# Written order on all engines, a new first stage for batch 0, and batch 1's q turned by TensorE, in a Linformer attention + maxout FFN kernel

## The chip, the cores and the metric

The kernel runs on one core of one Trainium2 chip. The metric is the time of one execution in microseconds (us). Lower is better. A kernel is timed in several rounds beside the kernel before, on the same chip. Runs are marked slow (a lower granted clock than the fast ones of the same kernel, and a time over 1.5% above the fastest). Ratios are taken from fast runs alone. "Span" is the time from the first to the last instruction in the profiled execution; it is about 2 us shorter than the time of that run. Engines: PE is TensorE's matmuls, PEld its weight loads, DVE is VectorE, ACT ScalarE, POOL GpSimd, SP the engine that issues to the hardware DMA queue.

## The reference

```python
# q, k, v: (8 batches, 8 heads, 1024, 64) fp32; E, F: (64, 1024); w1..w3: (512, 768); w_out: (768, 512)
k_proj = np.einsum('ks,bhsd->bhkd', E, k)
v_proj = np.einsum('ks,bhsd->bhkd', F, v)
attn = softmax(q @ k_proj^T / 8)            # over 64 projected keys
x = (attn @ v_proj) as (8192 tokens, 512)   # 1024 tokens per batch
out = max(x @ w1, x @ w2, x @ w3) @ w_out   # (8192, 512) fp32
```

## The kernel before: the parts that matter

TensorE works through the FFN of batch b, and between its steps it does the attention of batch b+1. One FFN batch is two halves ("chunks") of 512 tokens. Each half is six `up` steps of 12 matmuls and two `down` halves of 12. A `plan` says after which step which piece of attention comes. Only TensorE keeps the order in which the program is written. The framework that builds the program orders the other engines by its own estimate:

```python
ctx.enter_context(tc.manual_schedule(engines={mybir.EngineType.PE}))
...
def load(b):                                    # one buffer each for q, k, v
    dma = nc.gpsimd.dma_start(out=q_t, in_=view(q, b))   # waits for the transpose of batch b-1
    ...
    nc.gpsimd.dma_start(out=k_t, in_=view(k, b))         # fp32 in HBM, cast to bf16 on the way
    nc.gpsimd.dma_start(out=v_t, in_=view(v, b))

def q_by_dma(b):
    q_p = att.tile([P, NPAIR, SI, 2, D], BF16, name="q_p", bufs=1)
    for g in range(NPAIR):
        nc.vector.tensor_copy(out=q_p[:, g]..., in_=qkv[b][0][...])      # four VectorE copies
    qTs[b] = att.tile([P, NPAIR * SI, P], BF16, name="qT")               # two buffers
    last_T[b] = nc.sync.dma_start_transpose(out=qTs[b], in_=q_p...)

def up(b, ch, jt):
    ...                                          # 3 x 4 matmuls into three PSUM banks
    nc.scalar.copy(out=h1s, in_=h_ps[0])
    nc.vector.tensor_tensor(out=m12, in0=h_ps[1], in1=h1s, op=ALU.max)
    nc.vector.tensor_tensor(out=hTs[b, ch][:, jt, :], in0=h_ps[2], in1=m12, op=ALU.max)

def plan(b):
    ...
    (0, 0): [qd(n)],       # n = b + 1: q_by_dma(n) after the first up step of batch b
    (0, 2): [kv(n)], ...   # k and v projections
    (0, 3): [kt(n), ld(n + 1)], ...
```

The two maxima of `up` free the PSUM banks, and so let TensorE go on. If VectorE stands still, TensorE stops a few steps later.

The softmax here doesn't subtract the row's maximum and nothing guards it: scores larger than these inputs give would overflow.

## Time and profile before

| | before |
|---|---|
| time at the start, median of 3 | 464.06 us (460.72 to 464.39) |
| span of the profiled run | 460.0 us |
| PE, DVE, ACT busy | 88%, 43%, 44% |
| first FFN matmul | 28.2 us |
| end of batch 0 | 113.7 us |
| batches 1 to 7 | 50.8, 49.7, 51.8, 53.9, 47.2, 47.3, 41.4 us |

The end of a batch is the modelled end of its last `down` matmul in the timeline of PE. Batch 7 is shorter because there is no batch 8 to do attention for.

The windows view of the kernel before, two lines of one stretch each: busy us of each engine with the number of instructions, then granted clock, DMA share and GB/s. First batch 4, then batch 6:

```profile
266.00:319.90 53.90, 50.00 (x276) 22.95 (x274) 24.11 (x40) 24.27 (x47) 1.75 (x2) 0.94 0.57 123
...
367.10:414.40 47.30, 47.30 (x276) 21.11 (x274) 23.04 (x36) 24.27 (x46) 0.00 (x0) 1.00 0.11 46
```

The same 276 matmuls keep TensorE busy without a gap in batch 6 and leave 3.9 us open in batch 4; the other 2.7 us that batch 4 is longer are matmuls at a lower clock (0.94 on average against 1.00). Undisturbed, a batch takes 47.3 us, all of it TensorE.

VectorE's largest waits in the kernel before (engine, line, whom it waited for: us in total, times, longest):

```profile
DVE q_p L141 <- DMA q_t<-in_q_dram: 74.6, 7, 12.8
DVE xT L268 <- ACT zi L258: 35.9, 28, 2.7
```

The timeline of VectorE around one of the seven waits (start, duration, what; in brackets the idle time ahead of it and what ended it):

```profile
160.72 1.29 DVE L268 TENSOR_TENSOR xT<-bank,zi 128x512 bf16<-128x512 f32 x2 [1.21 <-ACT zi L258]
172.50 1.43 DVE L141 COPY q_p<-q_t 128x1024 bf16<-128x1024 bf16 x4 [10.49 <-DMA q_t<-in_q_dram]
173.85 0.69 DVE L294 TENSOR_TENSOR m_1421<-bank,h1s 128x512 f32<-128x512 f32 x1
```

VectorE stands 10.5 us before the four copies of a q that is still on its way. Batch 2's FFN began at 164.4 us; its first maxima (line 294) stand behind the copies until 173.9, although their matmuls were done at about 167. Two lines of PE's timeline show what this does to TensorE in batch 0 and in batch 2:

```profile
93.76 0.64 PE L225 MATMUL bank<-qT,kpT 64*64 64x512 bf16 x4 [14.14 <-DVE kpT L190]
...
174.59 1.06 PE L172 MATMUL bank<-k_t,eT 128*64 128x256 bf16 x16 [2.29 <-DVE m_1421 L294]
```

The chain of waits (start, us, what) shows why the load was late:

```profile
203.10 5.57 DMA qT<-q_p
208.70 0.04 POOLq L126
208.74 0.79 issue
209.55 13.15 DMA q_t<-in_q_dram
222.76 0.30 issue
223.07 1.09 DVE q_p L141 x3
224.16 0.61 DVE m_1919 L294
```

A q load starts when the preceding DMA transpose is done, and takes 13 us; then come the copies, then the FFN's maximum that had waited behind them.

### The profile page before, as it was taken

The page shows a single profiled execution, that of the slowest core. Times are in us where ns is not written, and L with a number is a line of the kernel's source. Part 1 is how long each engine was busy: PE and PEld are TensorE (multiplying, and loading weights), DVE is VectorE, ACT ScalarE, POOL GpSimd, SP SyncE. Part 2 cuts the span into 40 slices and gives each one's busy share as a digit, 9 for nine tenths or more (in the row PEclk, how much of TensorE's full clock was granted, in tenths as well). Part 3 has the DMA queues.
Part 4 walks back from the last instruction along what each step waited for, and adds up shares of the span by engine and source line. Part 5 has one row for each costly group of instructions (what it writes and reads, how often), then busy time and mean ns, then how long its engine had stood idle before and what let it go on. Part 6 is the DMA issues. An engine that isn't in the chain of part 4 may idle for free.

```text
span 460.0 us, 5849 instructions
## 1 busy us (share of the span) xinstructions
PE 406.3 (88%) x2272; PEld 181.7 (39%) x2272; DVE 197.2 (43%) x328; ACT 200.4 (44%) x377; POOL 33.0 (7%) x45
## 2 busy tenths in 40 slices
PE   1799298089889998999799988999999999999996
PEld 1334034034434444444444435444544454444442
DVE  1233234045273608362544607354535454554251
ACT  1434251049145633574155622656265625562322
POOL 6430000200100001000100001000100000000000
PEclk9999789579999999999899997999999999999999
DMA  8999867995892496727392485805391110101102
GB/s 142 197 194 207 146 120 167 167 172 137 157 164 93 91 184 89 187 66 131 89 173 91 97 179 81 179 27 152 52 198 48 46 47 19 74 27 65 62 30 92
DMA packets 67116, 53.33 MB, mean 116 GB/s; under 512 B 33168, under 2 KB 62608, under 8 KB 67088
## 3 DMA queue, kind: packets, MB, share of 16 engines
q0 software_dynamic: 33136, 28.31, 41.5%
q1 hardware_dynamic: 33952, 24.64, 16.7%
q8 instruction: 17, 0.28, 0.2%
q14 instruction: 11, 0.09, 0.1%
HBM read 57.15 MB, written 16.78 MB: 161 GB/s over the span
## 4 chain that ended last, share of the span: by engine, by line
PE 60%; DMA 29%; issue 4%; DVE 3%; ACT 2%; POOL 0%; POOLq 0%; DVEq 0%
PE bank L284 39%; DMA q_t<-in_q_dram 19%; PE bank L305 13%; DMA qT<-q_p 8%; PE bank L242 3%; DMA k_t<-in_k_dram 2%; PE bank L172 2%; PE bank L198 2%; PE bank L225 2%; DVE q_p L141 1%; ACT pT L235 1%; DVE hT L295 0%; ACT zl L256 0%; PE bank L156 0%; ACT zi L258 0%
## 5 line engine op out<-in xcount | busy, mean ns | idle before, releaser
L284 PE MATMUL bank<-xT,w_sb 128*128 128x512 bf16 x1152 | 266.1, 387 | 2.7 <-DVE m_950 L294 1.8
L284 PEld LDWEIGHTS <-w_sb 128*128 128x128 bf16 x1152 | 111.5, 99 | 148.3 <-issue 24.6
L292 ACT COPY h1s<-bank 128x512 f32<-128x512 f32 x96 | 56.4, 589 | 102.6 <-PE bank L284 82.1
L305 PE MATMUL bank<-wout_sb,hT 128*128 128x512 bf16 x384 | 85.8, 380 | 0.0
L235 ACT ACTIVATE pT<-bank 128x512 bf16<-128x512 f32 (+1 forms) x72 | 39.2, 598 | 48.3 <-PE bank L225 48.2
L268 DVE TENSOR_TENSOR xT<-bank,zi 128x512 bf16<-128x512 f32 x64 | 41.3, 686 | 36.3 <-ACT zi L258 35.9
L305 PEld LDWEIGHTS <-hT 128*128 128x128 bf16 x384 | 36.4, 98 | 47.9 <-issue 6.2
L256 ACT ACTIVATE zl<-bank 128x512 f32<-128x512 f32 x64 | 35.1, 597 | 42.7 <-PE bank L242 42.1
L312 ACT COPY o_sb<-bank 128x512 f32<-128x512 f32 x64 | 36.9, 593 | 27.9 <-PE bank L305 27.9
L141 DVE COPY q_p<-q_t 128x1024 bf16<-128x1024 bf16 x28 | 10.3, 422 | 74.6 <-DMA q_t<-in_q_dram 74.6
L258 ACT ACTIVATE zi<-zl 128x512 f32<-128x512 f32 x64 | 37.1, 632 | 0.0
L225 PE MATMUL bank<-qT,kpT 64*64 64x512 bf16 x128 | 16.3, 409 | 14.6 <-DVE kpT L190 14.4
L172 PE MATMUL bank<-k_t,eT 128*64 128x256 bf16 x128 | 10.8, 323 | 14.4 <-DMA k_t<-in_k_dram 5.3
L242 PE MATMUL bank<-pT,vp 64*64 64x512 bf16 x128 | 14.7, 396 | 9.1 <-DVE m_436 L294 8.6
L211 ACT CAST vp<-bank 64x256 bf16<-64x256 f32 x16 | 5.8, 364 | 33.8 <-PE bank L198 19.5
L242 PE MATMUL bank<-pT,ones 64*64 64x512 bf16 x128 | 17.6, 411 | 1.8 <-ACT pT L235 1.8
L126 POOL DMA_DIRECT2D q_t<-in_q_dram x7 | 6.1, 876 | 179.2 <-DVE hT L295 91.3
L172 PEld LDWEIGHTS <-eT 128*64 128x64 bf16 x128 | 8.5, 127 | 17.3 <-issue 17.2
L134 POOL DMA_DIRECT2D k_t<-in_k_dram x7 | 6.1, 876 | 103.7 <-PE bank L172 103.5
L213 DVE CAST vp<-bank 64x256 bf16<-64x256 f32 x16 | 6.8, 427 | 14.1 <-ACT vp L211 13.9
L225 PEld LDWEIGHTS <-kpT 64*64 64x64 bf16 x128 | 4.4, 109 | 20.8 <-DVE kpT L190 15.5
L242 PEld LDWEIGHTS <-ones 64*64 64x64 bf16 x128 | 4.8, 105 | 17.1 <-issue 17.0
(224 smaller groups left out, 203.5 us busy)
## 6 DMA issues: line engine op xcount, KB each, us to landing
out_dram<-o_sb SPq DMA_DIRECT2D x30, 512.0 KB, 2.7
k_t<-in_k_dram POOLq DMA_DIRECT2D x8, 1024.0 KB, 9.4
v_t<-in_v_dram POOLq DMA_DIRECT2D x7, 1024.0 KB, 13.5
q_t<-in_q_dram POOLq DMA_DIRECT2D x7, 1024.0 KB, 12.9
w_sb<-in_moe_w_dram POOLq DMA_DIRECT2D x6, 256.0 KB, 9.0
q_t<-in_q_dram POOLq DMA_DIRECT2D x2, 512.0 KB, 15.0
v_t<-in_v_dram POOLq DMA_DIRECT2D x2, 512.0 KB, 14.7
out_dram<-o_sb SPq DMA_DIRECT2D x4, 256.0 KB, 2.0
```

The costliest lines, as they stand in the source:

```text
L141: nc.vector.tensor_copy(out=q_p[:, g].rearrange("p si h d -> p h si d"), in_=qkv[b][0][:, 2 * g:2 * g + 2],)
L172: nc.tensor.matmul(out=ps[hh * HALF:(hh + 1) * HALF, 0:4 * D], lhsT=eT[:, si, :], rhs=qkv[b][1][:, 4 * hh:4 * hh + 4, si, :], start=(si == ...
L225: nc.tensor.matmul(out=sc[hp][c * HALF:(c + 1) * HALF, :], lhsT=kpTs[b][rows, g % 2, g // 2, :], rhs=qTs[b][rows, lo:lo + SPC, :], start=T ...
L235: nc.scalar.activation(out=pTs[b, g][r, hp, :], in_=sc[hp][r], func=AF.Exp, scale=scale)
L242: nc.tensor.matmul(out=dst[hp * HALF:(hp + 1) * HALF, :], lhsT=w(rows, hp), rhs=pTs[b, g][rows, hp, :], start=True, stop=True,)
L256: nc.scalar.activation(out=zl, in_=z[c], func=AF.Ln)
L258: nc.scalar.activation(out=zi, in_=zl, func=AF.Exp, scale=-1.0)
L268: nc.vector.tensor_tensor(out=xTs[b][:, g, c * SPC:(c + 1) * SPC, :].rearrange("a si p -> a (si p)"), in0=av[c], in1=zis.pop((b, g, c)), o ...
L284: nc.tensor.matmul(out=h_ps[i], lhsT=w_sb[i][:, ct, jt * P:(jt + 1) * P], rhs=rhs_x[:, ct, :, :], start=(ct == 0), stop=(ct == NCT - 1),)
L292: nc.scalar.copy(out=h1s, in_=h_ps[0])
L305: nc.tensor.matmul(out=o_ps, lhsT=hTs[b, ch][:, jt, tt * P:(tt + 1) * P], rhs=wout_sb[:, jt, :], start=(jt == 0), stop=(jt == NJT - 1),)
L312: nc.scalar.copy(out=o_sb[:, t, :], in_=o_ps)
```

## The change

The intent was to take the DMA-bound start apart (loads of batch 0 without a cast on the way, worked on by halves of the heads, with dummy matmuls to hold TensorE's clock), to turn batch 1's q by TensorE instead of copies and a DMA transpose, and to put every engine in written order. The diff, cut to its core:

```diff
-    ctx.enter_context(tc.manual_schedule(engines={mybir.EngineType.PE}))
+    ctx.enter_context(
+        tc.manual_schedule(engines={ET.PE, ET.DVE, ET.Activation, ET.Pool, ET.SP})
+    )
 ... (batch 0: fp32 loads through SP's queue)
+        nc.sync.dma_start(out=e_f, in_=E)
+        for i in range(2):
+            q_dma = nc.sync.dma_start(out=q_f[i], in_=view(q, 0)[:, hs[i], 0:SPC])
+        for i in range(2):
+            nc.sync.dma_start(out=k_f[i], in_=view(k, 0)[:, hs[i]])
+        nc.sync.dma_start(out=f_f, in_=F)
+        for i in range(2):                      # v still cast by GpSimd's queue, after q
+            dma = nc.gpsimd.dma_start(out=v_t[:, hs[i]], in_=view(v, 0)[:, hs[i]])
+            if i == 0:
+                after(dma, q_dma)
 ... (then weights, second half of q; its own casts, transposes, scores, sums, values)
+        idle(6)                                 # dummy matmuls; 17 in all
+        t = turn_ef(e_f)
+        nc.vector.tensor_copy(out=eT, in_=t)
+        idle(3)
 ... (ScalarE: exponentials wait until after the next up step's first copy)
+        nc.scalar.copy(out=h1s, in_=h_ps[0])
+        run_later()
 ... (plan of batch 0)
-                (0, 2): [sc(0, 0, c1), sc(0, 1, c1), qd(1)],
+                (0, 0): [qp(0, 0, c1), qp(0, 1, c1)],
+                (0, 1): [qp(0, 2, c1), qp(0, 3, c1), sc(0, 0, c1)],
 ...
-                (1, 1): [kv(1)],
-                (1, 2): [kt(1), sc(1, 0), ld(2)],
+                (1, 0): [kv(1)],
+                (1, 1): [do(turn_k, 1), qp(1, 0), qp(1, 1)],
+                (1, 2): [sc(1, 0), qp(1, 2), qp(1, 3), do(load, 2)],
 ... (plan of batch 1: batch 2's q copies and attention some steps later; loads of later batches one step earlier)
```

## The prediction

> **What bounds it now.** Undisturbed, TensorE bounds the kernel: the windows by batch show it busy 47.2 of 47.2 us in batch 5 and 47.3 of 47.3 in batch 6; batch 7 takes 41.5 us, then a tail of 4.1. The rest of the 460.0 us span is lost earlier:
>
> - Start to first FFN matmul: 28.2 us (timeline).
> - Batch 0: 28.2 to 113.5 us, with TensorE idle 8.6 us at 47.5 and 14.1 us at 79.6, and at about half clock around that (windows: 0.55 to 0.59).
> - Batches 1 to 4: 50.9, 49.7, 51.8, 53.9 us, 17.2 us over four times 47.27.
>
> The waits say why: VectorE waits 74.6 us in seven stalls for the q loads before its q_p copies. The automatic order put these copies ahead of the FFN's evictions, so a late load holds VectorE, then the banks, then TensorE. The load is late because its one buffer frees only after the preceding transpose: the chain of waits alternates q_t load (9.5 to 13.6 us) and transpose (5.3 to 7.3). Until about 54 us DMA is saturated: 19.4 MB of fp32 source (E, F, weights, batches 0 and 1) in about 52 us, 373 GB/s.
>
> **What the change does.**
>
> 1. Hand order: the copies of batch n come when their load, issued some 35 us earlier, is in. The 17.2 us of batches 1 to 4 go almost whole.
> 2. Batch 1's q by TensorE: one transpose leaves the DMA-bound front; it costs 2.1 us of TensorE (half as many take 1.08 now) and, with the order, removes the 8.6 and 14.1 us stalls, unless batch 1's loads are late.
> 3. Front: E, q, k come plain through the hardware queue, are cast on VectorE/ScalarE (0.4 to 1 us each) and worked by halves while v lands. The Trainium skill, "DMA: Bandwidth & Descriptors", section "Issuing engines are not separate DMA queues", says all queues share the same 16 engines; so no bandwidth is gained. 6.6 MB precede the first FFN matmul: 20.7 us at 373 GB/s plus 3 us; then v projection, values, multiply: first FFN matmul at 23.5 us.
> 4. Dummy matmuls keep the clock up. The skill, "TensorE: Matmul & The Clock Gate", Part 1, says idle TensorE falls to half clock; this trace agrees (0.43 us a matmul from 28.2 to 34 us, 0.22 later). Worth 3 us.
>
> **Sum (estimates).** First FFN matmul 23.5. Batch 0: twelve steps of 2.59 us, four downs of 2.6, attention of its second half and batch 1 about 9, ScalarE excess 3: ends near 78. k and v of batch 1 land about 49.4, needed 51; q 55, needed 55.5: tight. Then 6 x 47.27 + 41.5 + 4.1 = 329.2: span 407. Add 2 us from span to time and 2 us of order stalls (exponentials now wait behind the next h1s copy): 411 us. The gain, some 50 us, is all on TensorE's critical path; VectorE and ScalarE (43 and 44%) have room for the casts.
>
> Chances: faster by over 2% 0.96, within 2% 0.03, slower 0.01. Range 404 to 424.
>
> **Signs.** First FFN matmul at 22 to 26 us, at 0.22 us a matmul; no TensorE gap over 3 us after it; batch 0 done at 75 to 83; batches 1 to 6 at 47.3 to 48.3 each; VectorE's wait for q_t below 10 us; DMA as busy as now in the first 55 us.
>
> **What would make it wrong.** Batch 1's loads later than I count (a gap at 50 to 58 us); k delayed by v on the other queue, so ScalarE's exponentials start late; strict order costing ScalarE over 1 us per batch; another in-order wait on a DMA.

## The result

| | before | after |
|---|---|---|
| time, median of 4 | 464.23 us (460.72 to 464.81) | 417.01 us (415.92 to 417.56) |
| ratio | | 0.8994, 95% interval 0.8945 to 0.9043 |
| span | 460.0 us | 415.6 us |
| first FFN matmul | 28.2 us | 26.7 us |
| end of batch 0 | 113.7 us | 85.7 us |
| batches 1 to 7 | 50.8, 49.7, 51.8, 53.9, 47.2, 47.3, 41.4 | 48.5, 47.2, 47.3, 47.3, 47.3, 47.2, 41.5 |

A ratio is the mean time of one kernel's fast runs over that of the other's in the same rounds, so it is not quite the ratio of the medians.

The windows of the kernel after, batch 4:

```profile
228.60:275.90 47.30, 47.04 (x271) 21.16 (x275) 24.67 (x40) 25.21 (x46) 2.63 (x3) 1.00 0.64 134
```

The stall is gone (a few matmul records are missing in this trace, hence 271). VectorE's longest waits, and the group of the q_p copies (busy us, mean ns, then idle time just before them):

```profile
DVE xT L466 <- ACT zi L465: 46.5, 60, 2.5
DVE vp L410 <- ACT vp L408: 8.9, 14, 0.8
...
L329 DVE COPY q_p<-q_t 128x1024 bf16<-128x1024 bf16 x24 | 8.5, 420 | 0.0
```

The 74.6 us of waiting for q is now zero. On VectorE's timeline the copies stand behind the FFN's maxima and find their data landed:

```profile
137.17 0.69 DVE L500 TENSOR_TENSOR hT<-bank,m_1568 128x512 bf16<-128x512 f32 x1 [0.46 <-PE bank L488]
137.78 1.43 DVE L329 COPY q_p<-q_t 128x1024 bf16<-128x1024 bf16 x4
```

The front gained little. These are PE's first FFN step after, and the windows around it:

```profile
26.73 0.38 PE L488 MATMUL bank<-xT,w_sb 128*128 128x512 bf16 x1 [1.35 <-DMA w_sb<-in_moe_w_dram]
27.29 3.88 PE L488 MATMUL bank<-xT,w_sb 128*128 128x512 bf16 x10 [0.18 <-issue]
31.09 0.64 PE L345 MATMUL bank<-ident,q_t 128*64 128x128 bf16 x16
```

```profile
13.37:16.78 3.41, 1.59 (x29) 1.01 (x28) 1.56 (x3) 2.23 (x4) 1.77 (x3) 1.00 1.23 209
16.78:23.61 6.83, 5.83 (x52) 3.21 (x48) 2.83 (x6) 3.54 (x7) 3.71 (x5) 0.50 1.56 191
23.61:27.02 3.41, 1.54 (x17) 0.90 (x16) 2.40 (x5) 1.11 (x2) 1.55 (x3) 1.00 1.80 179
27.02:30.43 3.41, 3.23 (x9) 1.24 (x9) 0.28 (x1) 0.59 (x1) 3.41 (x5) 0.50 1.80 177
```

The clock was at half twice, from 16.78 to 23.61 us and from 27.02 to 30.43. The first time slowed the end of the front, the v projection above all. The second time slowed the first up step: 4.4 us (26.73 to 31.09) instead of 2.6. In the 3.41 us before each fall TensorE was busy 1.59 and 1.54 us.

### The profile page after: what moved, and what is told of

It is laid out like the page before. It is cut to its first block, busy times and chain, and to the rows that moved or that the text cites. A ratio compares the mean times of both kernels' runs of the same rounds, so it can differ in the third digit from the quotient of the medians.

```text
span 415.6 us, 6021 instructions
## 1 busy us (share of the span) xinstructions
PE 399.9 (96%) x2336; PEld 181.3 (44%) x2377; DVE 206.1 (50%) x337; ACT 207.8 (50%) x374; POOL 36.1 (9%) x49
## 3 DMA queue, kind: packets, MB, share of 16 engines
HBM read 57.15 MB, written 16.78 MB: 178 GB/s over the span
## 4 chain that ended last, share of the span: by engine, by line
PE 84%; ACT 6%; DMA 5%; issue 2%; DVE 1%; POOL 0%; SPq 0%
PE bank L488 55%; PE bank L510 19%; PE bank L444 4%; DMA v_t<-in_v_dram 3%; ACT zl L463 2%; ACT zi L465 2%; PE bank L363 2%; DMA q_f_91<-in_q_dram 2%; PE bank L391 1%; PE bank L424 1%; DMA w_sb<-in_moe_w_dram 1%; ACT pT L437 1%; PE bank L345 1%; ACT o_sb L517 0%; ACT h1s L496 0%
## 5 line engine op out<-in xcount | busy, mean ns | idle before, releaser
L488 PE MATMUL bank<-xT,w_sb 128*128 128x512 bf16 x1119 | 257.2, 381 | 3.4 <-DMA w_sb<-in_moe_w_dram 1.4
L488 PEld LDWEIGHTS <-w_sb 128*128 128x128 bf16 x1152 | 110.1, 98 | 139.4 <-issue 13.2
L466 DVE TENSOR_TENSOR xT<-bank,zi 128x512 bf16<-128x512 f32 x60 | 41.5, 692 | 46.5 <-ACT zi L465 46.5
L437 ACT ACTIVATE pT<-bank 128x512 bf16<-128x512 f32 (+1 forms) x64 | 34.8, 599 | 0.1
L444 PE MATMUL bank<-pT,ones 64*64 64x512 bf16 x120 | 15.0, 397 | 1.8 <-ACT pT L437 1.3
L83 POOL DMA_DIRECT2D w_sb<-in_moe_w_dram x18 | 13.6, 776 | 6.6 <-DMA v_t<-in_v_dram 4.7
L424 PE MATMUL bank<-qT,kpT 64*64 64x512 bf16 x120 | 14.2, 383 | 0.0
L329 DVE COPY q_p<-q_t 128x1024 bf16<-128x1024 bf16 x24 | 8.5, 420 | 0.0
L161 PE MATMUL two<-warm 128*128 128x512 bf16 x17 | 7.1, 542 | 1.2 <-DVE warm L140 1.2
L363 PE MATMUL bank<-k_t,eT 128*64 128x256 bf16 x112 | 7.4, 276 | 0.0
L391 PE MATMUL bank<-v_t,fT 128*64 128x256 bf16 x112 | 7.3, 273 | 0.0
## 6 DMA issues: line engine op xcount, KB each, us to landing
k_t<-in_k_dram POOLq DMA_DIRECT2D x7, 1024.0 KB, 14.1
```

The costliest lines, as they stand in the source:

```text
L83: nc.gpsimd.dma_start(out=wt[:, :, lo * P:hi * P], in_=w.rearrange("(ct p) j -> p ct j", p=P)[:, :, lo * P:hi * P],)
L363: nc.tensor.matmul(out=ps[hh * HALF:(hh + 1) * HALF, 0:4 * D], lhsT=eT[:, si, :], rhs=qkv[b][1][:, 4 * hh:4 * hh + 4, si, :], start=(si == ...
L424: nc.tensor.matmul(out=sc[hp][c * HALF:(c + 1) * HALF, :], lhsT=kpTs[b][rows, g, :], rhs=qTs[b][rows, lo:lo + SPC, :], start=True, stop=True,)
L437: nc.scalar.activation(out=pTs[b, g][r, hp, :], in_=sc[hp][r], func=AF.Exp, scale=scale)
L444: nc.tensor.matmul(out=dst[hp * HALF:(hp + 1) * HALF, :], lhsT=w(rows, hp), rhs=pTs[b, g][rows, hp, :], start=True, stop=True,)
L466: nc.vector.tensor_tensor(out=xTs[b][:, g, c * SPC:(c + 1) * SPC, :].rearrange("a si p -> a (si p)"), in0=av[c], in1=zi, op=ALU.mult,)
```

## The experiments

Each kernel was timed beside the kernel before; "ratio" is against it, in its own rounds. Two kernels of different rounds can only be compared roughly.

| run | what | median us | ratio (95%) |
|---|---|---|---|
| hand_only | before, all engines in written order | 421.26 | 0.916 (0.913 to 0.919) |
| q1_pe_auto | before, batch 1's q by TensorE | 458.69 | 0.997 (0.993 to 1.001) |
| auto_after | after, automatic order | 458.41 | 0.995 (0.991 to 1.000) |
| q1_dma | after, batch 1's q by DMA transpose | 416.27 | 0.904 (0.899 to 0.909) |
| hand_dve | before, VectorE in written order too | 428.68 | 0.926 (0.923 to 0.930) |
| hand_rest | before, all but VectorE in written order | 465.77 (two of 4 slow) | 0.998 (0.991 to 1.005) |
| old_front | after, with the front of before | 420.58 | 0.908 (0.906 to 0.911) |
| no_dummy | after, without dummy matmuls | 418.08 | 0.903 (0.900 to 0.905) |
| front_order | after, sums ahead in the front | 417.61 | 0.902 (0.899 to 0.906) |
| warm_late | after, 18 more dummy matmuls | 414.89 | 0.896 (0.893 to 0.900) |
| act_relief | after, eight copies on VectorE | 415.04 | 0.897 (0.894 to 0.901) |
| best | three of these together | 410.97 (one of 7 slow) | 0.889 (0.886 to 0.892) |

All results were correct. My theory was that the order is the gain. The rivals were batch 1's q (a shorter chain of load and transpose) and the new front.

### hand_only: the order alone

```diff
-    ctx.enter_context(tc.manual_schedule(engines={mybir.EngineType.PE}))
+    ctx.enter_context(tc.manual_schedule(engines={mybir.EngineType.PE, mybir.EngineType.DVE,
+        mybir.EngineType.Activation, mybir.EngineType.Pool, mybir.EngineType.SP}))
```

> The kernel before, with every engine in the order in which the program is written; nothing else. Theory 1 (the automatic order put the q_p copies and what follows too far ahead, and that is the loss): the 14.1 us gap and the stalls of batches 1 to 4 go, batches 1 to 6 take 47.3 to 48.5 us each, and the time falls to 424-434 us, that is most of the gain without any of the new code. Theory 2 (the gain comes from taking batch 1's q off the chain of load and DMA transpose): the stalls stay, 450 us or more. Theory 3 (the new front is the gain): about 460.

One line of the kernel before brings 421.26 us, even below what I expected. Batches 1 to 6 take 47.2 to 47.3 us each. One q wait is left, in batch 0:

```profile
DVE q_p L141 <- DMA q_t<-in_q_dram: 6.4, 1, 6.4
```

A listing of each engine's instructions in their order, without times, says where the copies stand. The table counts how many up steps (12 per batch) come before the q_p copies of each batch on VectorE:

| q_p copies of batch | 1 | 2 | 3 | 4 | 5 | 6 | 7 |
|---|---|---|---|---|---|---|---|
| automatic order (before) | 3 | 6 | 8-9 | 13-14 | 24 | 36 | 48 |
| written order (hand_only) | 3 | 13 | 25 | 37 | 49 | 61 | 73 |

The automatic order put the copies of batch 5 at the start of batch 2's FFN, two batches ahead of need. There is one q buffer, one q_p buffer and two qT buffers, so running ahead only turned each copy into a wait for the chain "qT buffer free, transpose, load". It also says why batches 5 and 6 of the kernel before were undisturbed: all seven copies had been done by then.

### q1_pe_auto: batch 1's q by TensorE, alone

```diff
-    (0, 2): [sc(0, 0, c1), sc(0, 1, c1), qd(1)],
+    (0, 2): [sc(0, 0, c1), sc(0, 1, c1)],
-    (1, 2): [kt(1), sc(1, 0), ld(2)],
+    (1, 2): [kt(1), q1(0), q1(1), sc(1, 0), q1(2), q1(3), ld(2)],   # q1: q_by_pe(1, g, 0 and 1)
```

> The kernel before in its automatic order, but batch 1's q turned by TensorE as after, not by the DMA transpose. Theory 1: the automatic order still hoists the q_p copies of later batches before the FFN's evictions, so batches 1 to 4 still lose some 10-17 us in all, and the time is 440-456 us. Theory 2: 420-430 us.

458.69 us, the same as before. The wait only moved: VectorE still waits 61.6 us for q, and TensorE has a gap of 7.6 us at 85 and one of 8.2 us at 127:

```profile
DVE q_p L141 <- DMA q_t<-in_q_dram: 61.6, 6, 12.7
```

My expected 440 to 456 us was a little too good; the theory stands, the rival (420 to 430) falls.

### auto_after: everything but the order

```diff
-        tc.manual_schedule(engines={ET.PE, ET.DVE, ET.Activation, ET.Pool, ET.SP})
+        tc.manual_schedule(engines={ET.PE})
```

> The kernel after, with only TensorE in written order, as before. Theory 1: VectorE again waits for q loads over 20 us in all, time 430-455 us. Theories 2 and 3: within 2% of 417 us.

458.41 us: without the order all the rest of the change is worth about 0.5% (ratio 0.995). The first FFN matmul is even later than before (32.6 us), and VectorE waits for q again:

```profile
DVE q_p L329 <- DMA q_t<-in_q_dram: 56.2, 6, 11.5
```

The time lies just above the range that I gave.

### q1_dma: the change without batch 1's q on TensorE

```diff
-        order = [(k_t, k), (v_t, v), (q_t, q)] if b == 1 else [(q_t, q), (k_t, k), (v_t, v)]
+        order = [(q_t, q), (k_t, k), (v_t, v)]
-                (0, 5): [za(0, 3, c1)],
+                (0, 5): [za(0, 3, c1), do(q_by_dma, 1)],
-                (1, 1): [do(turn_k, 1), qp(1, 0), qp(1, 1)],
-                (1, 2): [sc(1, 0), qp(1, 2), qp(1, 3), do(load, 2)],
+                (1, 1): [do(turn_k, 1)],
+                (1, 2): [sc(1, 0), do(load, 2)],
```

> The kernel after, but batch 1's q goes through copies and DMA transpose again, issued after the last up step of the first half of batch 0, with its load first of the three. Theory 1: in hand order the longer chain costs little; it saves TensorE 2.0 us of transposes and may wait a few us for k and v of batch 1, so 413-421 us. Theory 2: over 425 us.

416.27 us (412.87 to 417.83), as the theory expected: in written order the old way for batch 1 costs nothing, once its copies stand where the data has landed. Its profiled run, the fastest of the four, had batch 0 in 55.3 us against 59.0 after; 2.0 us of that are the transposes that TensorE no longer does and about 1.7 the clock, which was full from the first FFN matmul in that run. The timed runs don't show a clear gain.

### hand_dve and hand_rest: which engine's order

The edit is the same line, with PE and DVE in the set, or with all engines but DVE.

> The kernel before with TensorE (as it already was) and VectorE in written order; ScalarE, GpSimd and the DMA queue's engine stay in automatic order. Theory A (it is VectorE's order that loses the time): within 1.5% of hand_only's 421 us, 418-428 us, no q_p stall that holds TensorE after batch 0. Theory B (it is the order of the load issues and of ScalarE): over 445 us.

> The complement: the kernel before with every engine but VectorE in written order. Theory A: VectorE still stands at q_p copies before the FFN's evictions, 440-462 us. Theory B: 418-428 us.

hand_rest gives a ratio of 0.998: no gain. Its two fast runs took 459.9 and 464.3 us, the two slow ones 467.2 and 467.7. In its profile VectorE does the q_p copies of batches 2 to 7 some 7 to 10 up steps ahead of their written place, and waits for q:

```profile
DVE q_p L141 <- DMA q_t<-in_q_dram: 50.3, 7, 16.1
```

hand_dve gives 428.68 us, 0.7 us over my range. So VectorE's order carries about 34 of the gain (462.6 to 428.7), and the rest of the order some 7 us more on top of it (428.7 to 421.3, of different rounds), though it is worth nothing by itself. The batch ends place these 7 us in batch 0 (97.0 us in hand_dve, 90.3 in hand_only); all later batches take 47.2 to 47.3 us in both. GpSimd's timelines point to the cause, first hand_dve, then hand_only:

```profile
27.71 0.89 POOL L134 DMA_DIRECT2D k_t<-in_k_dram  x1 [0.18 <-PE bank L242]
29.01 0.88 POOL L135 DMA_DIRECT2D v_t<-in_v_dram  x1 [0.41 <-issue]
38.51 0.88 POOL L126 DMA_DIRECT2D q_t<-in_q_dram  x1 [8.62 <-PE bank L156]
```

```profile
38.13 0.88 POOL L126 DMA_DIRECT2D q_t<-in_q_dram  x1 [10.02 <-PE bank L156]
39.00 0.88 POOL L134 DMA_DIRECT2D k_t<-in_k_dram  x1
39.87 0.89 POOL L135 DMA_DIRECT2D v_t<-in_v_dram  x1
```

In the automatic order k and v of batch 1 go first and q lands behind them, at about 54 us; in written order q goes first and lands at 47.6. The copies stand at the same place, so VectorE waits 12.6 us in the one and 6.4 us in the other, and TensorE's gap behind it is 8.3 us and 2.5 us. ScalarE's order changed in the same step and was not tried alone.

### old_front: the change with the old front

The edit replaces the front by that of the kernel before (loads cast by GpSimd's queue, all heads at once, no dummies), in written order.

> The kernel after, but with the front of the kernel before (loads of batch 0 cast by GpSimd's queue, all heads at once, no dummy matmuls); hand order and batch 1's q on TensorE stay. If the new front is worth what first-FFN-matmul times say (28.2 or 28.8 against 26.7 us, and its cold first steps), 418.5-422 us, 0.4 to 1.2% slower than after; if the front is worth the 4.7 us and more of the prediction (28.2 to 23.5 us and 3 us of clock), 424 us or more; if nothing, 417.

420.58 us, and 418.08 for no_dummy in the same rounds. The first FFN matmul comes at 29.0 us instead of 26.7, and batch 0 ends at 88.1 instead of 85.7. The new front is worth 2.5 us (against no_dummy) to 3.6 us (against after, in other rounds).

### no_dummy: the dummy matmuls

```diff
         def idle(n):
+            return
```

> The kernel after without its 17 dummy matmuls. They end at 13.5 us, and the clock was at half again by 20 us in the profile of after, so I expect little: 416-419 us, first FFN matmul within 1 us of 26.7. The prediction's rival view (they keep the FFN's start warm, worth 3 us): 420 us or more.

418.08 us, first FFN matmul at 26.9 us, and the clock falls to half at 27.8 as it does after. The medians of no_dummy and after differ by 1.1 us, but they were not timed in the same rounds and the intervals of their ratios overlap: a gain from the 17 dummies as they stand is not shown.

### front_order: a guess that missed

```diff
         z0(0)
+        z0(1)
         kp = k_half(1)
-        z0(1)
 ...
         sc0(3)
-        v_half(0)
         z0(2)
-        av0(0)
         z0(3)
+        v_half(0)
+        av0(0)
         av0(1)
```

> The kernel after with four instructions groups of the front in another order: the sums of heads 2/3 right after those of 0/1, and those of the second half ahead of the v projection. In the profile of after ScalarE stood idle 1.1 us and 2.2 us for them, while VectorE's last multiply (done at 26.68) and a weight load (landed at 26.75 by the chain) both end at the first FFN matmul. If compute holds that matmul, it comes 1 to 1.5 us earlier and the time falls to 415.5-416.5 us; if the weight load does, nothing changes (417).

417.61 us, and the first FFN matmul came later, at 28.4 us. I had taken ScalarE's sums for the front's last wait. PE's timeline of this run shows another chain: v projection, VectorE's copy of it, the values, VectorE's multiply. My order had moved the v projection behind the sums:

```profile
24.06 1.89 PE L255 MATMUL two<-v_t,fT 128*128 128x256 bf16 x8
...
28.36 4.00 PE L488 MATMUL bank<-xT,w_sb 128*128 128x512 bf16 x9 [1.25 <-DVE xT L267]
```

This also helps with a doubtful line of the profile after: the first FFN matmul's wait was put down to a weight load landing at 26.75, but VectorE's last multiply ended at 26.68, and here a later multiply delays that matmul. GpSimd's timeline after speaks against the weight: the loads that the first up step reads were issued at 10.3 to 12.7 us, and the load in the chain, issued at 21.35, is one for the third up step.

### warm_late: dummies where TensorE waits

```diff
         sc0(1)
+        idle(2)
         z0(0)
+        idle(3)
         kp = k_half(1)
         z0(1)
+        idle(1)
         k_turn(1, kp)
+        idle(1)
 ...
         sc0(3)
+        idle(3)
 ...
         v_half(1)
+        idle(2)
         av0(2)
         av0(3)
+        idle(6)
```

> The kernel after with 18 more dummy matmuls, from the first scores to the end of the front, where TensorE waits anyway. If the front's end runs cold because TensorE was too little busy there, the first up step takes 2.6 instead of 4.3 us and the v projection 0.9 instead of 1.9: 414.5-416 us. If the clock does not follow this, or the dummies stand in the way, 417 or more.

414.89 us, within what I expected. The granted clock is recorded as 1.00 from 12 to 28 us, and the lengths of the matmuls agree: a v projection takes 1.05 us instead of 1.89, and the first FFN step goes at full speed:

```profile
25.94 2.75 PE L495 MATMUL bank<-xT,w_sb 128*128 128x512 bf16 x12
...
60.67 1.08 PE L352 MATMUL bank<-ident,q_t 128*64 128x128 bf16 x32 [1.28 <-DMA q_t<-in_q_dram]
```

The last line shows what takes part of this back in the profiled run: the first half of batch 0 ends 2.5 us earlier than after (52.1 against 54.6), but then TensorE waits 1.3 us for batch 1's q, and batch 0 ends only 0.9 us earlier. The intervals of the ratios of warm_late and after (other rounds) overlap, so the gain in time is not shown beyond doubt; the warm first step is. The same holds for the time of act_relief below.

### act_relief: ScalarE in batch 0's second half

In the profile after, steps that carry both exponentials and sums have more work on ScalarE than TensorE needs for them. The chain of waits after shows it:

```profile
72.33 0.57 ACT h1s L496
72.90 1.00 ACT pT L437 x2
73.90 0.04 issue
73.94 0.62 PE bank L444 x7
```

TensorE's sums wait for the exponentials, and those for the copy that was put ahead of them.

```diff
-        nc.scalar.copy(out=h1s, in_=h_ps[0])
+        (nc.vector.tensor_copy if (b, ch, jt) in ((0, 1, 4), (0, 1, 5)) else nc.scalar.copy)(
+            out=h1s, in_=h_ps[0]
+        )
-            nc.scalar.copy(out=o_sb[:, t, :], in_=o_ps)
+            (nc.vector.tensor_copy if (b, ch, half) in ((0, 1, 0), (1, 1, 0)) else nc.scalar.copy)(
+                out=o_sb[:, t, :], in_=o_ps
+            )
```

> The kernel after, but VectorE instead of ScalarE does eight copies: h1s of the last two up steps of batch 0, and the outputs of one down half of batches 0 and 1. If ScalarE is what TensorE waits for from 70 to 83 us and near 130 us (about 2.9 us and 1.2 us in the profile of after), batch 0 ends 2 to 3 us earlier, batch 1 takes 47.5 instead of 48.5, time 413-415.5 us. If VectorE becomes the new wait, 417 or more.

415.04 us. From the end of batch 1's first step with sums to the end of batch 0 (70.33 to 85.75 us after, 69.88 to 83.88 here) it takes 14.0 us instead of 15.4, and batch 1 takes 47.8 instead of 48.5. That is 2 us of the 3 to 4 that I hoped for; two waits of 0.31 us for VectorE's maxima are new.

### best: three edits together

The kernel after with the edits of q1_dma, warm_late and act_relief.

> The kernel after with three of the edits tried: batch 1's q by DMA transpose (2.0 us of TensorE less in batch 0), the late dummy matmuls, and the copies on VectorE instead of ScalarE. If they add up: first FFN matmul at 26 us and warm, batch 0 done at 79 us, batch 1 in 47.3-47.8, time 409-413 us, 1 to 2% under the 417 us of after. If the front's clock or batch 1's load of v takes it back, 414-417 us.

410.97 us, ratio 0.889. Six of its seven runs (409.88 to 414.55) lie below the fastest run of after (415.92); one, slow, took 417.77. Against after, in different rounds, that is 0.8889 / 0.8994, about 1.2% less. The profiled run was one of the slower ones. In it v of batch 1 came late, behind q and k:

```profile
57.73 1.92 PE L398 MATMUL bank<-v_t,fT 128*64 128x256 bf16 x16 [2.56 <-DMA v_t<-in_v_dram]
```

How often the faster runs have that wait too is open: they have no profile.

## Why the prediction was right

The predicted time of 411 us was 6 us short of the measured 417, within the range. Point by point:

- **Written order ends the stalls of batches 1 to 4: right.** The predicted gain was 17.2 us. Batches 1 to 4 went from 206.2 us to 190.3 (sums of the table), 15.9 us less. hand_only, with nothing but the order, has all of it and more (189.0), and auto_after, with all but the order, has none of the gain. hand_dve and hand_rest show that it is VectorE's order. The Trainium skill, "TensorE: Matmul & The Clock Gate", table of specifications, calls the queues of ScalarE, VectorE and GpSimd strictly first in, first out. This trace agrees for VectorE: it stood 10.5 us before a copy whose data had not landed, and matmuls finished at about 167 us had to wait behind that copy until 173.9.
- **Batch 1's q by TensorE, "with the order, removes the 8.6 and 14.1 us stalls": only the order did.** hand_only has no wait of TensorE over 2.5 us in batch 0, and q1_dma costs nothing. This part of the change was not needed.
- **The front: wrong in size.** The text said: "first FFN matmul at 23.5 us". It was 26.7. I had counted the data (20.7 us) and a short tail. v's second half landed at 20.3 us by the chain of waits, near enough, but the chain around it (two v projections, the first at half clock, copies, values, multiplies) ran from 20.05 to 26.68 us, against the 2.8 us that I gave it.
- **"Dummy matmuls keep the clock up ... Worth 3 us": wrong.** They end at 13.6 us; the clock fell to half at 16.8, rose at 23.6, and fell again at 27.0, just after the first FFN matmul, so the FFN's first step took 4.4 us instead of 2.6. warm_late, with dummies up to that matmul, took 2.75 us. The prediction left out that the clock could fall again between the dummies and the FFN. (q1_dma has the front of after, and its clock did not fall the second time: 2.75 us too. What decided it is open.)
- **"Attention of its second half and batch 1 about 9": too small.** Summing PE's timeline from step to step gives 12.1 us: 1.1 for the transposes of q's second half, 3.6 for scores, sums and values of that half, 1.9 for k and v, 2.6 for turning k and q with the first scores, and about 2.9 for the rest at its unhindered length. "ScalarE excess 3" was right: the stretch from 70.33 to 85.75 us holds 12.5 us of TensorE work, at its unhindered length, in 15.4.
- **The sum.** End of batch 0 predicted 78, measured 85.7: 3.2 us from the front, 1.8 from the clock and 3.1 from the attention make 8.1, within half a microsecond. From there to the end 329.2 was predicted and 329.9 measured (415.6 - 85.7). The whole miss is in the first batch; of the 2 us that were added for order stalls, the later batches needed 0.7.
- **Batch 1's loads, "k and v ... about 49.4, needed 51; q 55, needed 55.5": in time by luck.** From issue and time to landing, v came at 51.4 us and q at 56.5, both later than predicted. No wait followed, since TensorE itself came 6 us later than predicted (k and v at 57.1, q at 61.8). In the profiled runs of warm_late and best, where the first half of batch 0 ends 2.5 to 3 us earlier and the last of these loads lands later (q at 60.6 us in the one, v at 57.7 in the other), TensorE does wait, 1.3 and 2.6 us.
- **The signs.** Those of the later batches came true: no gap over 3 us, and no wait for q_t. Those of the front did not: first FFN matmul at 26.7 us (22 to 26 forecast) and not at full speed, batch 0 done at 85.7 (75 to 83).
- **No bandwidth gained by the other queue: right.** The prediction cited the Trainium skill, "DMA: Bandwidth & Descriptors", section "Issuing engines are not separate DMA queues". The windows after show 402 GB/s landed while fp32 comes in plain (10 to 12 us), and 178 to 206 GB/s from 16 to 30 us, when it is cast to half the bytes on the way, which is an estimated 356 to 412 GB/s read if all of it is cast. The kernel before, with nearly all of its loads cast, landed 199 to 207 GB/s from 10 to 18 us, an estimated 398 to 414 read. The source rate is about the same, and old_front shows that the front as a whole was worth only about 3 us.

## What to carry to other kernels

When an engine waits long for a load and another engine stops because of it, first look at where the waiting instruction stands in that engine's order, before making the load faster: one line of ordering took the time from 460.7 to 421.3 us here, and the rewritten front and the new path for q only on to 417.0 (other rounds). An automatic order that runs ahead was harmful here, where buffers are single, since the early instruction waited for its own predecessor's buffer and held everything behind it. Whether a second q buffer would have helped the automatic order was not tried. The dummy matmuls that kept the first FFN step at full speed ran up to the moment at which it was needed; those that ended 13 us earlier did not.

## What the Trainium skill lacked or had wrong

- "TensorE: Matmul & The Clock Gate", Part 1, gives about 3.4 us of idleness in its table as what halves the clock. Here it fell twice, at 16.8 and 27.0 us, with no idle gap over 1.4 us since 1.2 us; TensorE was busy 1.59 and 1.54 us of the 3.41 us before. The page itself reports a kernel in which short idles were enough ("A second HAM failure mode"), but not how much work is enough, and busy time alone does not tell it: in q1_dma the clock fell after 3.41 us with 2.62 us busy (13.48 to 16.89) and did not fall after 3.41 us with 1.67 us busy (23.71 to 27.12). With the gaps filled (warm_late: 11.97 us busy of the 13.6 from 13.4 to 27.0) it did not fall.
- The same page warns that the clock's records can't be fully trusted, without this case: until the first change is recorded, the profile shows 1.00 while the clock is at half. In the kernel before it shows 1.00 from 28.2 to 34 us, where the weight loads come every 0.43 us (0.22 us later); after, the first six dummy matmuls took 2.74 us at a recorded 1.00.
- "DMA: Bandwidth & Descriptors", Specifications, gives about 358 GB/s as the HBM limit of a core and names no condition in that row. This kernel runs on one core, and the windows of after and of q1_dma show 402 GB/s landed from HBM (10 to 12 us and 5 to 10 us). The condition stands further down: the section "Bandwidth" of the same page gives about 358 for each of two cores that stream at once, and up to 425 for one core alone. So only the row is incomplete.
- No page that I read treats the order of instructions on VectorE and GpSimd as a cost of its own: 462.6 us became 428.7 with VectorE in written order and nothing else.
